# Features of tiles 2 and 3 made and turned in the spatial stage, features of tiles 6 and 7 turned by VectorE: a two-branch mixer in float32 on one core

## The chip, the cores and the metric

The kernel runs on one core of a Trainium2 chip. Its engines are TensorE (PE in the profile; PEld is its weight load), VectorE (DVE), ScalarE (ACT), GpSimd (POOL) and SyncE (SP), which issues most transfers; GpSimd issues some, too. Each engine works its own list of instructions in order. The metric is the device time of one execution in microseconds (us), lower is better, as the median of the runs shown.

## The reference

x is 2048 x 512. Two branches read its layer norm, and their sum is added to x:

```
xn = layernorm(x)
# branch A: 32 heads of width 16
q, k, v = split(xn @ wqkv)
phi_q = concat(softmax(q @ w_phi), softmax(-(q @ w_phi)))       # 32 features for each head; phi_k alike
num = phi_q @ (phi_k^T v);  den = phi_q . sum(phi_k) + 1e-6
A = (num / den) @ wo
# branch B: 688 + 688 features
z1, z2 = gelu(xn @ w_in) split in two;  z2 = layernorm(z2)
g = w_sp @ z2 + b_sp                                            # w_sp is 2048 x 2048, over the sequence
B = (z1 * g) @ w_out
out = x + A + B
```

## The kernel before

Rows of x are cut into 16 tiles of 128 (NT). Every float32 product that must be exact is made of three matmuls: an operand is split into a rounded part (by ScalarE, line 49, or by a copy) and a rest (by VectorE, line 53), and `mm3` (lines 57 to 59) adds high x high, high x low and low x high.

**First stage**: projections, softmax features of q and k for each tile. The unfinished features of q (the exponentials and their sums) go to the DRAM array `e_d`, the first half of branch B to `z1_d`.

**Spatial stage** (its matmuls start between 275.4 and 484.0 us of the span): g = w_sp @ z2. Output rows are done in 8 row pairs i = 0 to 7 (256 rows each), and each pair in four steps over the sequence, so that there are 32 steps n (NC; SEQ gives pair and quarter). A step is a 2x2 block product with seven instead of eight products (FORM: P1 to P7); each is 6 matmuls, 42 in a step, added up over the four steps of a pair in seven PSUM tiles `g` out of a pool of 8. For each step a raw block of w_sp comes in by SyncE (`load_a`, line 607, tile `wf`), and `prep_a` makes its operands `A` from it: ScalarE rounds (line 49), VectorE takes four rests (line 53) and four sums and differences (lines 637 to 640). The operands of steps n and n + 2 share a buffer. At the end of a pair, `drain` adds up the seven products into `c` (lines 834 to 840 on VectorE), and `gate` multiplies by gelu(z1) (line 850 on ScalarE, 853 on VectorE), splits a remainder, and turns the result: VectorE transposes blocks of 32x32 (line 862 twice, line 864), and eight transfers on SyncE (lines 868, 870) store it so that it reads back as whole transposed blocks (`u_d`, `ur_d`). The tile that holds gelu(z1) and then the turned result is `z1t`, one buffer; `c` is one buffer, too. `load_z1` (line 808, GpSimd) fills `z1t` for the next pair.

**Output stage** (to the end): for each pair of tiles TensorE multiplies u by w_out (`project_u`), the features of q by phi_k^T v (`attend`, line 1062, PSUM `po`), and the result by wo (`project_o`). The features of a tile s must be finished first (`q_fin`, lines 563 to 570: a product, a sum over each head, five small steps, a product, all on VectorE) and turned so that features lie on partitions. Turning is done in two ways:

- TensorE transposes (`attend_T`, line 1047, tile `ptq`, 16 for a pair of tiles), and ScalarE copies the result from PSUM (line 1049, four for a pair);
- VectorE transposes blocks (`turn_q`, line 579), four transfers on GpSimd store them to the DRAM array `q_d` (line 581), and SyncE loads them turned (line 1012).

Before, tiles 0 and 1 are finished ahead of the spatial stage (NE = 2), and turned by VectorE in it, behind the gates of pairs 2 and 4 (lines 963 to 968); tile 2 is finished at step 29; tiles 3 to 15 are finished in the output stage (`features`), three tiles ahead of their use. Tiles from TQ = 8 on are turned by VectorE, so that TensorE transposes the pairs of tiles 2 and 3, 4 and 5, 6 and 7.

The code is recorded in program order, and a scheduler sorts the instructions of each engine by a timing of its own; `in_turn` adds an order by hand for the steps at the start of the spatial stage, and `tc.issue_after` holds an instruction behind another one.

## Time and profile before

| | us |
|---|---|
| median of 3 runs (610.21 to 615.73) | 610.74 |
| the profiled execution, its own time | 612.24 |
| its span, from the first to the last instruction | 610.5 |

| engine | busy in the span |
|---|---|
| TensorE | 602.8 us (99%) |
| its weight loads | 548.5 us (90%) |
| VectorE | 525.4 us (86%) |
| ScalarE | 260.3 us (43%) |
| GpSimd | 131.8 us (22%) |

A row of the timeline gives the start in us, the duration (of all that is merged in the row), the engine, the line, the operation, output and input tiles with their shapes, the count, and in brackets the idle time before it and what ended that. Spans of neighbouring instructions on one engine can overlap by up to 0.1 us, so the step from start to start is what an instruction costs in a full queue. An instruction that waits holds all that stands behind it on its engine.

### The profile page before, as it was taken

To read this page: it belongs to the slowest core of one execution; us is meant where nothing else is said; L and a number is where in the kernel's file an instruction comes from. 1 tells how busy PE (TensorE), PEld (TensorE's weight loads), DVE (VectorE), ACT (ScalarE), POOL (GpSimd) and SP (SyncE) were. 2 spreads that over 40 slices of the span, in tenths; PEclk is the share of its full clock that TensorE was granted. 3 is DMA by queue.
4 is the path that set the end of the run, shared out by engine and by line. 5 is a ranking of instruction groups with operands and counts; after the bars stand their busy time and mean duration, and the time that the engine had idled before them with its cause. 6 is when DMAs were issued, how large, how long until landed. Compare 5 with 4: busy or idle time off the path is not lost.

```text
span 610.5 us, 11382 instructions
## 1 busy us (share of the span) xinstructions
PE 602.8 (99%) x4286; PEld 548.5 (90%) x4286; DVE 525.4 (86%) x930; ACT 260.3 (43%) x414; POOL 131.8 (22%) x231
## 2 busy tenths in 40 slices
PE   8999999999999999999999999999999999999997
PEld 7888888888888999999999999999999988877775
DVE  5999999999987578989999897997998999999922
ACT  5643324423433547877434433443435343332220
POOL 4122332323111005442000001001100041153420
PEclk9999999999999999999999999999999999999999
DMA  8557876566537758002344736556664799699782
GB/s 315 193 130 178 217 176 188 145 168 165 144 96 221 241 201 306 5 1 65 121 107 135 208 104 173 163 154 161 176 185 154 228 299 292 191 326 248 183 236 67
DMA packets 57950, 107.85 MB, mean 177 GB/s; under 512 B 12392, under 2 KB 24552, under 8 KB 57672
## 3 DMA queue, kind: packets, MB, share of 16 engines
q1 hardware_dynamic: 43656, 65.22, 34.6%
q0 software_dynamic: 11936, 36.28, 24.2%
q10 hardware_dynamic: 2304, 5.64, 2.4%
q8 instruction: 33, 0.54, 0.4%
q14 instruction: 21, 0.17, 0.1%
HBM read 66.85 MB, written 35.54 MB: 168 GB/s over the span
## 4 chain that ended last, share of the span: by engine, by line
PE 82%; DVE 5%; ACT 4%; issue 4%; POOL 3%; DMA 1%; ACTq 0%; POOLq 0%; DVEq 0%
PE g L57 9%; PE g L59 9%; PE g L58 9%; PE proj L58 7%; PE proj L57 7%; PE proj L59 7%; PE pout L57 5%; PE pout L59 5%; PE pout L58 5%; PE zps L57 3%; PE zps L59 3%; PE zps L58 3%; PE po L1062 1%; DMA et<-e_d 1%; PE kvps L372 1%
## 5 line engine op out<-in xcount | busy, mean ns | idle before, releaser
L57 PE MATMUL g<-B,A 128*128 128x344 f32 x448 | 140.4, 317 | 0.9 <-ACT A L49 0.9
L58 PE MATMUL g<-B,A 128*128 128x344 f32 x448 | 141.1, 317 | 0.0
L59 PE MATMUL g<-B,A 128*128 128x344 f32 x448 | 135.5, 317 | 0.0
L49 ACT ACTIVATE A<-wf 128x512 fp32r<-128x512 f32 (+1 forms) x128 | 69.9, 573 | 109.5 <-DVE wf L639 64.8
L57 PEld LDWEIGHTS g<-B,A 128*128 128x128 f32 x448 | 83.8, 188 | 1.4 <-ACT A L49 1.4
L53 DVE TENSOR_TENSOR A<-wf,A 128x512 fp32r<-128x512 f32 (+1 forms) x128 | 76.5, 619 | 9.8 <-ACT A L49 9.4
L58 PEld LDWEIGHTS g<-B,A 128*128 128x128 f32 x448 | 84.0, 188 | 0.0
L59 PEld LDWEIGHTS g<-B,A 128*128 128x128 f32 x448 | 82.7, 188 | 0.3 <-DVE A L53 0.2
L57 PE MATMUL proj<-wqk_h,xT 128*128 128x512 f32 x128 | 50.1, 391 | 0.0
L59 PE MATMUL proj<-wqk_h,xT 128*128 128x512 f32 x128 | 49.8, 389 | 0.0
L58 PE MATMUL proj<-wqk_l,xT 128*128 128x512 f32 x128 | 49.8, 389 | 0.0
L124 ACT ACTIVATE e<-e,r_x 128x1024 f32<-128x1024 f32 x26 | 29.7, 1148 | 42.2 <-DVE e L123 41.2
L57 PE MATMUL zps<-w1h,xT 128*128 128x344 f32 (+2 forms) x128 | 40.9, 320 | 0.0
L59 PE MATMUL zps<-w1h,xT 128*128 128x344 f32 (+2 forms) x128 | 40.7, 318 | 0.0
L58 PE MATMUL zps<-w1l,xT 128*128 128x344 f32 (+2 forms) x128 | 40.7, 318 | 0.0
L57 PE MATMUL zps<-w2h,xT 128*128 128x344 f32 (+2 forms) x128 | 40.7, 318 | 0.0
L58 PE MATMUL zps<-w2l,xT 128*128 128x344 f32 (+2 forms) x128 | 40.6, 317 | 0.0
L59 PE MATMUL zps<-w2h,xT 128*128 128x344 f32 (+2 forms) x128 | 40.3, 317 | 0.0
L127 DVE TENSOR_REDUCE sm<-e 128x64 f32<-128x1024 f32 x26 | 31.1, 1199 | 2.5 <-ACT e L124 2.5
L808 POOL DMA_DIRECT2D z1t<-z_d x16 | 9.1, 594 | 105.3 <-DVE A L53 38.2
L57 PE MATMUL pout<-wu,uh 128*128 128x512 f32 x75 | 30.4, 406 | 0.0
L59 PE MATMUL pout<-wu,ul 128*128 128x512 f32 x75 | 29.3, 391 | 0.0
(217 smaller groups left out, 1373.0 us busy)
## 6 DMA issues: line engine op xcount, KB each, us to landing
wf<-in_wst SPq DMA_DIRECT2D x64, 256.0 KB, 3.8
e_d<-e POOLq DMA_DIRECT2D x16, 544.0 KB, 4.4
et<-e_d SPq DMA_DIRECT2D x16, 544.0 KB, 7.1
z_d<-z1f ACTq DMA_DIRECT2D x16, 344.0 KB, 2.9
z1t<-z_d POOLq DMA_DIRECT2D x16, 344.0 KB, 4.2
zacc<-e POOLq DMA_DIRECT2D x10, 512.0 KB, 4.8
u<-u_d SPq DMA_DIRECT2D x15, 320.0 KB, 4.9
xt<-in_x SPq DMA_DIRECT2D x16, 256.0 KB, 4.3
```

The lines of the kernel that those rows point to most:

```text
L49: return act.activation(h, src, AF.Copy).ins
L53: return (eng or dve).tensor_tensor(l, src, h.bitcast(F32), op=ALU.subtract).ins
L57: pe.matmul(dst, ah, bh, start=start, stop=False)
L58: pe.matmul(dst, ah, bl, start=False, stop=False)
L59: return pe.matmul(dst, al, bh, start=False, stop=stop).ins
L124: softmax_pair.last = less, act.activation(e, e, AF.Exp, scale=scale).ins
L127: dve.tensor_reduce(sm, heads(e), axis=AX.X, op=ALU.add)
L372: i = pe.matmul(kv_acc[k:k + QP, m // 4], vs[:, m * QP:(m + 1) * QP], e[:, m * HP:(m + 1) * HP], start=first and m < 4 and len(ready) == n ...
L808: pool.dma_start(t[:, k, :FH], z1_d[2 * i + k])
L1062: lasts[3] = pe.matmul(po[r][c * QP:(c + 1) * QP, k], kvT[rows, m // 2, cols], fs[m // 4][rows, m // 2 % 2], start=True, stop=True).ins
```

## The change

- `if 0 < i < 5` in place of `if i in (2, 4)`: behind the gates of pairs 1, 2, 3 and 4 the features of tiles 2, 0, 3 and 1 are turned. Tiles 2 and 3 (s >= NE) are finished there, too: their exponentials are loaded into `c` by GpSimd, and `q_fin` runs with `z1t` as its scratch and with `zs`, a copy of the denominators' sums.
- `zs` takes the third buffer of the raw blocks (`wfy`) from step 6 on; raw blocks from n = 8 on have two buffers, and from n = 6 on `load_a(n + 4)` stands behind `prep_a(n + 2)` in the program.
- TQ = 6: tiles 6 and 7 are turned by VectorE. `ft[2]` is loaded turned, and at step 29 tile 4 is finished instead of tile 2. TensorE then transposes one pair, that of tiles 4 and 5. In the output stage `features` runs from tile 5 on, five tiles ahead.
- `in_turn` gets gate 0's parts, and a second call orders the parts of `prep_a` of steps 8 to 31 one behind another.

```
-    TQ = 8
+    TQ = 6
...
-        tag = "fx"[n] if n < 2 else "fxy"[(n - 2) % 3]
+        tag = "fx"[n] if n < 2 else "fxy"[(n - 2) % 3] if n < 8 else "fx"[n % 2]
...
-        if n + 4 < NC:
+        if n < 6:
             raw[n + 4] = load_a(n + 4)
         if 0 < n < NC - 2:
             A[n + 2] = prep_a(n + 2, raw.pop(n + 2))
+        if 6 <= n < NC - 4:
+            raw[n + 4] = load_a(n + 4)
+        if n == 6:
+            zs = fy[0].tile([P, 2, QC, P], F32, tag="wfy", name="zs").rearrange("p a b c -> p (a b c)")
+            pool.dma_start(zs, zb_d)
...
-                    (4, "A11"), (4, "A22"), (4, "first"), (4, "sums"),
+                    (4, "A11"), (4, "A22"), ("c12", 0), (4, "first"), (4, "sums"),
...
-                    (6, "A11"), (6, "A22"), (6, "first"), (6, "sums"), (6, "S2"), (6, "S4"),
+                    (6, "A11"), (6, "A22"), ("z", 0), (6, "first"), (6, "sums"), (6, "S2"), (6, "S4"),
+                    ("u", 0),
                     (7, "A11"), (7, "A22"), (7, "first"), (7, "sums"), (7, "S2"), (7, "S4"),
+                    ("ut", 0, 0), ("ut", 0, 1),
                     (8, "A11"), (8, "A22"), (8, "first"), (8, "sums"), (8, "S2"), (8, "S4"))
...
-            if i in (2, 4):
-                s = i // 2 - 1
-                e, t = (gt.tile([P, 2, FU], F32, tag=tag, name=name).rearrange("p k f -> p (k f)")[:, :NF]
+            if 0 < i < 5:
+                s = (2, 0, 3, 1)[i - 1]
+                e, t = (gt.tile([P, 2, FU], F32, tag=tag, name=name).rearrange("p k f -> p (k f)")
                         for tag, name in (("c", "c"), ("z1", "z1t")))
-                pool.dma_start(e, e_d[s, :, :NF])
+                t = t[:, :NF]
+                if s < NE:
+                    e = e[:, :NF]
+                    pool.dma_start(e, e_d[s, :, :NF])
+                else:
+                    e, _ = q_fin(load_q(s, e[:, :QW], pool), t, zs)
                 turn_q(s, t, e, pool)
...
-            ets[2] = load_q(2, slot("et"))
-            es[2], last = q_fin(ets.pop(2), slot("qtmp")[:, :NF], zb)
+            ets[4] = load_q(4, slot("et"))
+            es[4], last = q_fin(ets.pop(4), slot("qtmp")[:, :NF], zb)
...
+    in_turn(*((n, k) for n in range(8, NC) for k in ("A11", "A22", "first", "sums", "S2", "S4")))
...
-        ets[3] = load_q(3, slot("et"))
-        for s in (2, 3):
-            us[s] = fetch_u(s)
-        ets[4] = load_q(4, slot("et"))
+        ets[5] = load_q(5, slot("et"))
+        us[2] = fetch_u(2)
+        ft[2] = f_pair()
+        for k in range(2):
+            sp.dma_start(ft[2][:, k], q_d[2 + k])
+        us[3] = fetch_u(3)
+        ets[6] = load_q(6, slot("et"))
...
-        if 3 < i + 3 < NT:
-            features(i + 3)
+        if 0 < i < NT - 5:
+            features(i + 5)
```

From line 849 on the changed kernel's numbers are higher: the gate's 853, 862 and 864 read 854, 863 and 866 there.

**VectorE, behind the gate of pair 1, before.** Here stand the last block of the gate's transposes (L864) and the operands of the next steps, those of two steps mixed:

```order
L864 STREAM_TRANSPOSE z1t<-c 128x192
L639 TENSOR_TENSOR wf<-wf 128x2x128
L640 TENSOR_TENSOR wf<-wf 128x2x128
L53 TENSOR_TENSOR A<-wf,A 128x2x256 x2
L53 TENSOR_TENSOR A<-wf,A 128x256
L637 TENSOR_TENSOR wf<-wf 128x2x128
L53 TENSOR_TENSOR A<-wf,A 128x2x256
L638 TENSOR_TENSOR wf<-wf 128x2x128
L53 TENSOR_TENSOR A<-wf,A 128x256
L639 TENSOR_TENSOR wf<-wf 128x2x128
L637 TENSOR_TENSOR wf<-wf 128x2x128
L640 TENSOR_TENSOR wf<-wf 128x2x128
```

The same place now, from the end of the operands' second difference (L638) on:

```order
L638 TENSOR_TENSOR wf<-wf 128x2x128
L563 TENSOR_TENSOR z1t<-c,zs 128x1024
L639 TENSOR_TENSOR wf<-wf 128x2x128
L564 TENSOR_REDUCE c<-z1t 128x64
L640 TENSOR_TENSOR wf<-wf 128x2x128
L53 TENSOR_TENSOR A<-wf,A 128x2x256
L565 TENSOR_TENSOR c<-c 128x64
L53 TENSOR_TENSOR A<-wf,A 128x2x256
L566 SCALAR_TENSOR_TENSOR c<-c 128x32
L53 TENSOR_TENSOR A<-wf,A 128x2x256
L53 TENSOR_TENSOR A<-wf,A 128x256
L567 RECIPROCAL c<-c 128x32
```

The seven instructions that finish tile 2 have come in between the operands of two steps, the first of them (L563) four instructions into a step's sums.

**VectorE, on to the drain of pair 2.** The rows that follow a little later in the changed kernel; L834 and L837 are the first two steps of the drain of pair 2:

```order
L568 TENSOR_TENSOR c<-c 128x64
L638 TENSOR_TENSOR wf<-wf 128x2x128
L570 TENSOR_TENSOR c<-c 128x1024
L639 TENSOR_TENSOR wf<-wf 128x2x128
L579 STREAM_TRANSPOSE z1t<-c 128x1024
L640 TENSOR_TENSOR wf<-wf 128x2x128
L53 TENSOR_TENSOR A<-wf,A 128x2x256
L834 SCALAR_TENSOR_TENSOR c<-g,bias,c 128x344
L837 TENSOR_TENSOR c<-g,c 128x344
```

All of the finishing and the turning (L579) thus stands ahead of the drain of pair 2, in a stretch where there was nothing of it.

**TensorE, end of the first pair of tiles in the output stage, before** (`ptq` is the PSUM tile of the transposes, `woh` and `wol` are wo, `wu` is w_out):

```order
L57 MATMUL pout<-woh,oT 128x512
L58 MATMUL pout<-wol,oT 128x512
L59 MATMUL pout<-woh,oT 128x512
L1047 MATMUL ptq<-ident,et 128x128 x16
L57 MATMUL pout<-wu,uh 128x512
L58 MATMUL pout<-wu,uh 128x512
L59 MATMUL pout<-wu,ul 128x512
```

and now:

```order
L57 MATMUL pout<-woh,oT 128x512
L58 MATMUL pout<-wol,oT 128x512
L59 MATMUL pout<-woh,oT 128x512
L57 MATMUL pout<-wu,uh 128x512
L58 MATMUL pout<-wu,uh 128x512
L59 MATMUL pout<-wu,ul 128x512
```

The block of 16 transposes is gone here; it is gone, too, behind the pair of tiles 4 and 5, and stays behind that of tiles 2 and 3.

More of the change, by code (lines that the diff above doesn't have):

```diff
@@ L553, in mixer, with load_q @@
     QW = NF + 7 * H
-    def load_q(s, et):
-        sp.dma_start(et[:, :NF + 2 * H], e_d[s])
+    def load_q(s, et, eng=None):
+        (eng or sp).dma_start(et[:, :NF + 2 * H], e_d[s])
         return et
@@ L648, in in_turn @@
         for e in range(2):
-            queue = [turns[k][e] for k in keys if e < len(turns[k])]
+            queue = [turns[k][e] for k in keys if e < len(turns[k]) and turns[k][e]]
             for a, b in zip(queue, queue[1:]):
@@ L844, in drain @@
             turns["c", i, k] = x.ins,
+        turns["c12", i] = None, first.ins
         return cb, first.ins, drained.ins
@@ L849, in gate @@
         with tc.issue_after(after or first):
-            act.activation(z[:, :, :FH], z[:, :, :FH], AF.Gelu_apprx_tanh)
+            turns["z", i] = None, act.activation(z[:, :, :FH], z[:, :, :FH], AF.Gelu_apprx_tanh).ins
         zs = z[:, :, :FH].rearrange("p k (j f) -> p k j f", j=2)
         us = u[:, :, :FH].rearrange("p k (j f) -> p k j f", j=2)
-        dve.tensor_tensor(us, zs, cb, op=ALU.mult)
+        turns["u", i] = dve.tensor_tensor(us, zs, cb, op=ALU.mult).ins,
         lo, hi = u[:, :, KF * P:FH], u[:, :, FH:FU].bitcast(F32R)
@@ L861, in turn @@
             for k in range(2):
-                dve.transpose(m[:, k * KF * P:(k + 1) * KF * P].rearrange("p (m c t) -> p m c t", c=KF, t=BL),
-                              u[:, k, :KF * P].rearrange("p (c m j) -> p m c j", c=KF, j=BL))
+                turns["ut", i, k] = dve.transpose(
+                    m[:, k * KF * P:(k + 1) * KF * P].rearrange("p (m c t) -> p m c t", c=KF, t=BL),
+                    u[:, k, :KF * P].rearrange("p (c m j) -> p m c j", c=KF, j=BL)).ins,
             dve.transpose(r.rearrange("p (k f) -> p k f", k=2), u[:, :, KF * P:])
@@ L1123, in mixer @@
     with tc.issue_after(load_w.last):
-        ets[3] = load_q(3, slot("et"))
-        for s in (2, 3):
-            us[s] = fetch_u(s)
-        ets[4] = load_q(4, slot("et"))
+        ets[5] = load_q(5, slot("et"))
[5 more added lines that the diff above has]
+        ets[6] = load_q(6, slot("et"))
     def ahead(i):
-        if i + 5 < NT:
-            ets[i + 5] = load_q(i + 5, slot("et"))
+        if i + 7 < NT:
+            ets[i + 7] = load_q(i + 7, slot("et"))
         if i + 4 < NT:
-            with tc.issue_after(brought[i + 2]) if i + 6 >= NT else ExitStack():
+            with tc.issue_after(brought[i + 4]) if i + 6 >= NT else ExitStack():
                 us[i + 4] = fetch_u(i + 4)
-        if 3 < i + 3 < NT:
-            features(i + 3)
+        if 0 < i < NT - 5:
+            features(i + 5)
     p, nxt = {}, dict(enumerate(uT))
@@ L1153, in mixer @@
             fin.append(lasts[7])
-            features(3)
+            features(5)
             with tc.issue_after(fin[-1]), tc.issue_after(lasts[8]):
```

## The prediction

> **What bounds the kernel now.** I read the page first, then the queue of TensorE, then stretch by stretch what VectorE has left.
>
> ```profile
> PE 602.8 (99%) x4286; PEld 548.5 (90%) x4286; DVE 525.4 (86%) x930; ACT 260.3 (43%) x414; POOL 131.8 (22%) x231
> ...
> PE g L57 <- ACT A L49: 0.9, 2, 0.6
> ...
> 580.78 1.06 issue
> ```
>
> TensorE is busy 99% of the span. The view of waits finds 0.9 us at two places of the spatial stage, the chain of work 1.06 us at 580.78, ahead of the products with the turned features (L1062). So TensorE is the bound, and what is taken off it is gained, as long as nobody makes it wait instead. The page's 86% for VectorE is a mean over stages; I look at the stage that gets new work. A row pair is four steps of 42 matmuls:
>
> ```profile
> L57 PE MATMUL g<-B,A x448: 313/316/427, 275.4 to 483.7; 128*128 128x344 f32 x150
> ...
> L59 PE MATMUL g<-B,A x448: 313/316/429, 275.7 to 484.0; 128*128 128x344 f32 x150
> ```
>
> These are 3 x 448 = 1344 matmuls between 275.4 and about 484.1 us; less some 1.7 us of gaps that is 0.154 us each, 6.47 us a step and **25.9 us a row pair**. I cut the stage into stretches of 25.9 us, from drain to drain of pairs 1 to 5:
>
> ```profile
> 324.10:350.00 25.90, 25.90 (x170) 25.90 (x169) 24.14 (x53) 12.27 (x22) 1.19 (x3) 1.00 0.57 167
> 350.00:375.90 25.90, 25.90 (x170) 25.90 (x169) 20.22 (x39) 8.32 (x15) 1.86 (x4) 1.00 0.49 133
> 375.90:401.80 25.90, 25.90 (x170) 25.85 (x169) 24.22 (x52) 11.35 (x21) 3.06 (x6) 1.00 0.63 168
> 401.80:427.70 25.90, 25.90 (x170) 25.90 (x169) 21.27 (x41) 9.99 (x19) 2.67 (x5) 1.00 0.54 153
> ```
>
> The fourth number of busy times is VectorE's (behind the length, PE and PEld): 24.14, 20.22, 24.22 and 21.27 of 25.9 us. TensorE never stops here, at a granted clock of 1.00. VectorE has 13.75 us left in 103.6, and even that isn't all free:
>
> ```profile
> 350.32 0.58 DVE L834 SCALAR_TENSOR_TENSOR c<-g,bias,c 128x344 f32<-128x344 f32 x1 [0.70 <-PE g L59]
> ...
> 373.03 1.25 DVE L579 STREAM_TRANSPOSE z1t<-c 128x1024 f32<-128x1024 f32 x1 [3.36 <-DMA wf<-in_wst]
> ...
> 378.14 0.57 DVE L834 SCALAR_TENSOR_TENSOR c<-g,bias,c 128x344 f32<-128x344 f32 x1
> ...
> 402.55 0.57 DVE L834 SCALAR_TENSOR_TENSOR c<-g,bias,c 128x344 f32<-128x344 f32 x1
> ...
> 424.02 1.25 DVE L579 STREAM_TRANSPOSE z1t<-c 128x1024 f32<-128x1024 f32 x1 [2.50 <-DMA wf<-in_wst]
> ...
> 429.13 0.57 DVE L834 SCALAR_TENSOR_TENSOR c<-g,bias,c 128x344 f32<-128x344 f32 x1
> ```
>
> The L834 rows are the first additions of the drains of pairs 2, 3, 4 and 5. At 350.32 VectorE was ahead and waited for TensorE. From there its own stretches are 27.8, 24.4 and 26.6 us. Those of 27.8 and 26.6 hold a turning (L579), before which it stood 3.36 and 2.50 us: the tile `z1t` has to be free of the gate's eight stores, and the exponentials to have come in. The stretch of 24.4 us holds no turning. So VectorE is itself within 2 us of the bound here, and at 378.14 it was 1.9 us behind TensorE's pace (350.32 + 25.9 = 376.2) without stopping it.
>
> **The change, part by part.**
>
> *Off TensorE.* Two of three blocks of transposes go:
>
> ```profile
> 498.76 1.75 PE ptq L1047 x16
> ...
> 531.18 1.75 PE ptq L1047 x16
> ```
>
> That is 2 x 1.75 = **3.5 us** of the chain. The eight copies that ScalarE no longer makes of them cost nothing (it is busy 43%). The 1.06 us at 580.78 go, too: features are finished five tiles ahead instead of three, and VectorE has two finishings fewer in the output stage for two turnings more. **Gain 4.6 us.** The transfers there grow, by my count, by four turned tiles loaded and two stored for two fewer loads of exponentials; between TensorE's use and the landing lies the longer lead, so I cost them at nothing, and at up to 2 us if that cover is too short.
>
> *Onto VectorE.* Finishing a tile is seven instructions:
>
> ```profile
> L563 DVE TENSOR_TENSOR qtmp<-et,zb x16: 1217/1218/1228, 220.0 to 572.9; 128x1024 f32<-128x1024 f32 x16
> L564 DVE TENSOR_REDUCE et<-qtmp x16: 1177/1210/1221, 222.3 to 575.9; 128x64 f32<-128x1024 f32 x16
> ...
> 516.47 1.22 DVE L563 TENSOR_TENSOR qtmp<-et,zb 128x1024 f32<-128x1024 f32 x1
> ...
> 521.24 1.22 DVE L563 TENSOR_TENSOR qtmp<-et,zb 128x1024 f32<-128x1024 f32 x1
> ```
>
> From one tile's first instruction to the next tile's first, with nothing else between, 4.77 us; between other work the gaps are filled, and I take 4.6. The turning adds 1.2 (L579: 1.25, overlapping), and the wait before it is now before L563, which writes `z1t`: it stands about as far behind the gate's transposes as L579 did, so I take the mean of 3.36 and 2.50, 2.9. Against that, the new instructions stand between those of the operands, where some waiting was:
>
> ```profile
> 345.72 0.42 DVE L639 TENSOR_TENSOR wf<-wf 128x256 f32<-128x256 f32 x1
> 346.05 0.42 DVE L637 TENSOR_TENSOR wf<-wf 128x256 f32<-128x256 f32 x1
> ...
> 355.89 0.42 DVE L637 TENSOR_TENSOR wf<-wf 128x256 f32<-128x256 f32 x1
> 356.35 0.43 DVE L638 TENSOR_TENSOR wf<-wf 128x256 f32<-128x256 f32 x1
> ...
> 322.88 1.29 DVE L53 TENSOR_TENSOR A<-wf,A 128x512 fp32r<-128x512 f32 x2 [0.32 <-ACT A L49]
> ```
>
> An instruction that doesn't need the one ahead of it starts 0.33 us after it, one that does 0.46; a step's third rest waits 0.32 us for ScalarE's rounding. Four such gaps of 0.12 and two waits of 0.32 are filled: 1.1 us less. The Trainium skill, page "VectorE: DVE Perf Modes", section "The DRAIN you can't avoid", says that the next operation does not start until the pipe has emptied, and that chaining operations without semaphores wins nothing. The two spacings above differ by 0.13 us, so this trace does not bear it out; by the rule alone the 1.1 would be 0.6, and the sum 1 us higher.
>
> A stretch with finishing and turning (pairs 1 and 3) therefore takes VectorE 24.4 + 4.6 + 1.2 + 2.9 - 1.1 = **32.0 us**. A stretch with a turning alone (pairs 2 and 4) took 27.8 and 26.6, mean **27.2 us**. But in these a wait is new, because the stretch ahead of each now turns, too:
>
> ```profile
> 374.57 2.22 POOL L581 DMA_DIRECT2D q_d<-z1t  x4 [7.66 <-DVE wf L639]
> 381.28 1.10 POOL L808 DMA_DIRECT2D z1t<-z_d  x2 [4.50 <-DMA wf<-in_wst]
> ...
> 387.12 1.34 ACT L850 ACTIVATE z1t<-z1t 128x1376 f32<-128x1376 f32 x1
> ...
> z1t<-z_d POOLq DMA_DIRECT2D x16, 344.0 KB, 4.2
> ```
>
> From the turning's start (373.03) it is 8.3 us to the next issue of gelu's input (381.28), 0.5 to its second half, 4.2 to landing, 1.3 for gelu: 14.3 us. In the changed order there stand between the turning and the gate's multiply the turning itself (1.2), the seven additions of a drain (402.55 to 407.36 in the timeline, less two rests between them: 3.6), the operands of one step and a half (4.4 and 2.4): some 11.7 us. The wait is between 0 and 2.6 us; I take the middle, 1.3 for each of the two stretches. Behind the waiting multiply stand the operands of the next steps, and TensorE waits for those.
>
> Sum: 2 x 32.0 + 2 x 27.2 + 2 x 1.3 = 121.0 us for VectorE where TensorE needs 103.6: **17.4 us too much**. How much VectorE may be late before TensorE stops is not shown, except that 1.9 did no harm. The other end is the PSUM pool: eight tiles, seven of them in use, so a product's tile is written again eight products later, 7.4 us after the product began and 6.5 after it ended (a product takes 0.92), less the 0.57 of L834: 5.9. I take 4.5, nearer the second end, since the first is only what happened to occur; not the whole 5.9, since a step's operands follow each other with less room than the drain has. **TensorE loses 17.4 - 4.5 = 12.9 us.** The two stretches behind pair 4 hold no new work and don't give the time back, since TensorE can't be faster than its matmuls.
>
> Ends of this term: if all other waits of VectorE vanish (13.75 free less 2 x 2.9 standing gives 7.9) the excess is 2 x 4.6 + 2 x 1.2 + 2 x 2.9 - 7.9 = 9.5, less 5.9: a loss of 3.6. If none vanishes, nothing is filled and the multiply waits 2 x 2.6: 17.4 + 5.2 - 1.9 = 20.7.
>
> *Costed at nothing.* Two raw buffers instead of three: a raw block lands 3.8 us after its issue by the page, and the operands of one step in between take 4.4 us (318.50 to 322.88 in the timeline):
>
> ```profile
> wf<-in_wst SPq DMA_DIRECT2D x64, 256.0 KB, 3.8
> ...
> 318.50 2.23 DVE L53 TENSOR_TENSOR A<-wf,A 128x512 fp32r<-128x512 f32 x4 [0.30 <-ACT A L49]
> ```
>
> It is close, and up to 1 us a step where operands follow each other with nothing between; that is in stretches with room. Gate 0's multiply behind later operands may win the 0.9 us of waits near 318, but VectorE is then as late as before; nothing, or -0.9.
>
> Sum for the profiled execution: 612.24 - 4.6 + 12.9 = 620.5 us (its span is 1.7 us shorter). It lay 1.5 us above the median of 610.74, so on the median: **619.0 us**.
>
> **Rivals.**
>
> 1. *VectorE absorbs it; the gain of TensorE stays.* For it: TensorE is at 99% and VectorE at 88% in the four stretches, and 3.36 + 1.2 us too much did no harm in one of them. Against it: the four sums above, with every stretch over 25.9. It decides by whether the excess stays below what may be late, some 5.9 us. The time: 610.74 - 4.6 = 606.1 us, faster. The Trainium skill, page "Perfetto Trace Analysis", section "Identifying the Most-Contended Engine", says to optimize the engine of highest occupancy first; by it this rival wins, and the page's 99% against 86% agree with it as far as they go.
> 2. *It nearly cancels.* The low end of VectorE's term, 3.6 to 7 us lost for 4.6 won: 609.7 to 613.1 us. For it speaks that ScalarE's waits shrink when VectorE is late.
> 3. *Worse than forecast.* Full waits at the multiply, raw blocks late in the catching up as well, nothing tolerated beyond 1.9: 610.74 - 4.6 + 20.7 = 626.8 us.
> 4. *The transposes don't go.* The order of TensorE shows two blocks of 16 fewer, so I give it no chance.
>
> **How the numbers follow.** Forecast 0.60, with its own range of 613 to 625 (a loss of 7 to 19 us); rival 1 0.14; rival 2 0.18; rival 3 0.08. Leaving out rival 3 and most of rival 1 leaves out 2 in 10: the range is 607 to 625 us. A difference of 1% (6.1 us) is about what a measurement of this kernel can tell from no change. Faster by over 1% (below 604.6) lies outside all cases: 0.04. Slower by over 1% (above 616.9) is three quarters of the forecast and rival 3: 0.53. Within 1% remains 0.43.
>
> **What would show it.** In the changed kernel's profile TensorE should have gaps of 5 us and more in all ahead of the drains of pairs 2 and 4 and smaller ones ahead of those of pairs 3 and 5, released by ScalarE's rounding, VectorE's rests or the drain; VectorE should be busy over 95% there, standing about 3 us at L563 twice and at L579 twice, and at the gate's multiply of pairs 2 and 4. The chain of work should show one `ptq` block, and no wait before L1062 at the pair of tiles 12 and 13. I am wrong if TensorE stays gapless to 484 us (then rival 1), if the wait at L563 is below 1 us, or if TensorE waits in the output stage for turned features.

## The result, and the profile after

The changed kernel takes **635.49 us** (median of 5 runs, 635.15 to 636.63), the kernel before on the same chip 611.35 (5 runs, 610.21 to 615.73): a ratio of **1.0388**, 95% interval 1.0362 to 1.0415. It is slower by 24.1 us, where 8.3 were forecast and 625 was the upper end of the range. The profiled execution took 636.63 us, its span 634.9.

The first part of the page (busy time, share of the span), and the view of what TensorE waited for in the spatial stage:

```profile
PE 610.7 (96%) x4254; PEld 549.5 (87%) x4254; DVE 527.9 (83%) x934; ACT 253.3 (40%) x406; POOL 142.8 (22%) x250
```

```profile
PE g L57 <- ACT A L49: 12.6, 11, 2.8
PE g L57 <- ACT c L835: 2.5, 2, 1.8
PE g L59 <- DVE A L53: 0.7, 2, 0.4
```

TensorE, at 99% before, is at 96%. In the spatial stage it now waits 12.6 us at 11 places for ScalarE's rounding of an operand (L49), and 2.5 us for the drain's first copy out of PSUM (L835), where it waited 0.9 us in all before. The next view cuts the stage from the first matmul of a pair to the first of the next (pairs 2 to 7; behind the length stand the busy times of PE, PEld, DVE, ACT and POOL, then the granted clock):

```profile
328.80:356.20 27.40, 26.43 (x170) 25.87 (x169) 23.21 (x48) 9.39 (x17) 1.60 (x3) 1.00 0.49 141
356.20:385.60 29.40, 26.95 (x169) 26.00 (x169) 24.11 (x47) 10.50 (x19) 5.24 (x10) 1.00 0.55 152
385.60:418.70 33.10, 28.68 (x171) 27.34 (x170) 26.57 (x56) 9.49 (x17) 2.48 (x5) 0.95 0.53 155
418.70:447.90 29.20, 26.70 (x170) 26.14 (x170) 22.40 (x44) 9.95 (x18) 3.85 (x7) 0.99 0.57 159
sum 119.10, PE 108.75 PEld 105.36 DVE 96.29 ACT 39.33 POOL 13.18; mean PE 27.19 PEld 26.34 DVE 24.07 ACT 9.83 POOL 3.29
...
447.90:476.40 28.50, 27.74 (x169) 27.17 (x169) 22.28 (x46) 10.02 (x18) 4.39 (x8) 0.95 0.55 146
476.40:510.20 33.80, 29.06 (x170) 27.65 (x169) 29.51 (x58) 15.19 (x28) 0.00 (x0) 0.95 0.67 209
```

A pair that took 25.9 us takes 27.4, 29.4, 33.1, 29.2, 28.5 and 33.8. But VectorE is not at its limit: 96.3 us of 119.1 in pairs 2 to 5, or 81%. The last product ends at 510.4 us, against 484.3 before: **26.1 us later** (the stage begins 0.9 later). The output stage behind it gives back 1.6 us: 124.7 us instead of 126.3. For all the pairs, from the starts of the 1344 matmuls of both traces: the gaps of over 0.4 us hold 17.8 us more than before, matmuls spaced at 0.25 to 0.4 us instead of 0.154 hold 6.4 us more.

VectorE's own waits, from 318 to 515 us:

```profile
DVE A L53 <- ACT A L49: 13.4, 17, 4.2
DVE c L854 <- ACT z1t L851: 6.8, 6, 2.3
DVE z1t L563 <- DMA wf<-in_wst: 6.1, 2, 3.3
DVE z1t L579 <- DMA wf<-in_wst: 2.7, 1, 2.7
```

It stands before the finishing (L563), the turning (L579) and the gate's multiply (L854), about as long as was forecast, and 13.4 us for roundings that ScalarE was late with. (ScalarE waits in its turn, mostly for VectorE's sums, and 13.9 us at six places for raw loads, where before it was 0.2 us at one.) So where does the time go? The chain of work from 337 to 371 us shows it (start, length, what); the row above it is the gate's multiply, with its first and last start in that window:

```profile
L854 DVE TENSOR_TENSOR c<-z1t,c x2: 1591/1592/1593, 337.0 to 370.7; 128x1376 f32<-128x1376 f32 x2
```

```profile
341.94 0.29 DVE z1t L866
...
345.00 3.99 DMA ur_d<-z1t
...
349.27 1.23 DVE z1t L563
...
355.81 1.13 DVE c L570
...
357.28 0.81 DVE z1t L579
...
364.90 0.46 POOL z1t L808
...
365.45 3.62 DMA z1t<-z_d
...
369.33 1.36 ACT z1t L851
370.72 1.59 DVE c L854
```

The stores of the turned tile, one of the steps, aren't in this chain; they are in the row of GpSimd's timeline:

```profile
358.73 2.23 POOL L581 DMA_DIRECT2D q_d<-z1t  x4 [15.35 <-DVE z1t L579]
```

From one gate's multiply to the next are **33.7 us**, and the rows go round two buffers, `c` and `z1t`, that exist once each. Gate and its turning into `z1t` (L866 ends at 342.2): 5.2 us. The gate's stores have to land before `z1t` may be written: to 349.0, 6.8 us. Finishing (L563 to L570, between preparations), to 356.9: 7.9 us. Turning into `z1t`: to 358.4, 1.5 us. The turned tile's stores, until the load of the next gate's input may be issued (L808): 6.5 us. (The chain puts the end of this wait down to a raw load. But L808 waits for the four stores, too: the last of them landed at 364.1 us, and in all four turnings L808 begins 0.6 to 0.8 us after that landing.) That load: to 369.3, 4.4 us. Gelu: 1.4 us. No engine is full in it; it is a ring of steps that wait for each other, longer than the 25.9 us in which TensorE does a pair. With a turning and no finishing it is shorter, in the next pair 27.3 us (370.72 to 398.01). How much of the loss hangs on this ring, the runs below have to show.

### The profile page after: what moved, and what is told of

Read it like the earlier page. It is cut to its first block, busy times and chain, and to the rows that moved or that the text cites. A ratio compares the mean times of both kernels' runs of the same rounds, so it can differ in the third digit from the quotient of the medians.

```text
span 634.9 us, 11370 instructions
## 1 busy us (share of the span) xinstructions
PE 610.7 (96%) x4254; PEld 549.5 (87%) x4254; DVE 527.9 (83%) x934; ACT 253.3 (40%) x406; POOL 142.8 (22%) x250
## 4 chain that ended last, share of the span: by engine, by line
PE 60%; DVE 18%; DMA 13%; issue 4%; ACT 3%; SPq 2%; POOL 0%; DVEq 0%; ACTq 0%; POOLq 0%
PE proj L58 7%; PE proj L57 7%; PE proj L59 7%; DMA wf<-in_wst 6%; PE zps L59 6%; PE zps L58 6%; PE zps L57 6%; PE g L57 3%; PE g L59 3%; PE g L58 3%; DVE A L53 3%; PE pout L57 3%; PE pout L59 3%; PE pout L58 3%; DMA u<-u_d 2%
## 5 line engine op out<-in xcount | busy, mean ns | idle before, releaser
L57 PE MATMUL g<-B,A 128*128 128x344 f32 x448 | 144.8, 326 | 15.1 <-ACT A L49 12.6
L49 ACT ACTIVATE A<-wf 128x512 fp32r<-128x512 f32 (+1 forms) x128 | 66.6, 569 | 122.6 <-DVE wf L639 101.0
L57 PEld LDWEIGHTS g<-B,A 128*128 128x128 f32 x448 | 85.6, 191 | 19.5 <-ACT A L49 15.8
L53 DVE TENSOR_TENSOR A<-wf,A 128x512 fp32r<-128x512 f32 (+1 forms) x128 | 74.3, 617 | 18.3 <-ACT A L49 18.0
L58 PEld LDWEIGHTS g<-B,A 128*128 128x128 f32 x448 | 85.9, 192 | 0.0
L59 PEld LDWEIGHTS g<-B,A 128*128 128x128 f32 x448 | 81.8, 191 | 2.5 <-DVE A L53 2.4
L127 DVE TENSOR_REDUCE sm<-e 128x64 f32<-128x1024 f32 x26 | 31.1, 1198 | 2.5 <-ACT e L124 2.5
L581 POOL DMA_DIRECT2D q_d<-qtmp x40 | 22.6, 577 | 37.7 <-DVE qtmp L579 37.7
L59 PE MATMUL pout<-wu,ul 128*128 128x512 f32 x75 | 29.3, 390 | 0.0
```

Source lines behind the costliest of these rows:

```text
L49: return act.activation(h, src, AF.Copy).ins
L53: return (eng or dve).tensor_tensor(l, src, h.bitcast(F32), op=ALU.subtract).ins
L57: pe.matmul(dst, ah, bh, start=start, stop=False)
L58: pe.matmul(dst, ah, bl, start=False, stop=False)
L59: return pe.matmul(dst, al, bh, start=False, stop=stop).ins
L127: dve.tensor_reduce(sm, heads(e), axis=AX.X, op=ALU.add)
```

## The experiments

Theories, as they came up. **RING**: the lost third raw buffer. **WORK**: VectorE's added instruction time, as forecast. **ORDER** and **LIST**: TensorE's new order of products, and the list that causes it. **TURNS**: the two turnings more with their waits, whatever the list. **WAIT**: VectorE's in-order queue held ahead of finishing and turning. **CHAIN** (first called CYCLE): the ring of steps through `c` and `z1t`, some of which are transfers. Each time stands beside runs of the kernel before on the same chip, whose medians were 611.2 to 611.9 us.

### Undoing and doing single parts

The raw ring of two alone, on the kernel before:

```diff
-        tag = "fx"[n] if n < 2 else "fxy"[(n - 2) % 3]
+        tag = "fx"[n] if n < 2 else "fxy"[(n - 2) % 3] if n < 8 else "fx"[n % 2]
 ...
-        if n + 4 < NC:
+        if n < 6:
             raw[n + 4] = load_a(n + 4)
         if 0 < n < NC - 2:
             A[n + 2] = prep_a(n + 2, raw.pop(n + 2))
+        if 6 <= n < NC - 4:
+            raw[n + 4] = load_a(n + 4)
```

> The kernel before, with one part of the change alone: from step 8 on the raw row blocks go round two buffers instead of three, so that a block's load is issued only after the block two steps earlier has been read. Nothing is finished or turned in addition. If the lost third buffer is what costs (theory RING), VectorE's ordinary work should already run into late loads: 615 to 628 us, with TensorE gaps that end on wf<-in_wst in pairs 2 to 7. If VectorE's added finishing and its waits cost (theory WORK), the loads land in time as the prediction said: 611 to 613 us. If TensorE's new product order costs (theory ORDER), 611 to 612, since its order is here nearly that of before.

620.9 us, ratio 1.0159 (1.0137 to 1.0182). ScalarE's and TensorE's waits in its spatial stage:

```profile
ACT A L49 <- DMA wf<-in_wst: 49.5, 21, 5.3
...
PE g L57 <- ACT A L49: 3.7, 4, 1.9
PE g L59 <- DVE A L53: 1.6, 1, 1.6
```

ScalarE waits for raw loads at 21 places (0.2 us at one place before), and TensorE for ScalarE. By itself this edit, which the prediction costed at nothing, costs **9.4 us**, in the band of RING. But that is not the change's price. Three raw buffers again in the changed kernel, the copy of zb gone from the third:

```diff
-        tag = "fx"[n] if n < 2 else "fxy"[(n - 2) % 3] if n < 8 else "fx"[n % 2]
+        tag = "fx"[n] if n < 2 else "fxy"[(n - 2) % 3]
 ...
-                    e, _ = q_fin(load_q(s, e[:, :QW], pool), t, zs)
+                    e, _ = q_fin(load_q(s, e[:, :QW], pool), t, e[:, :NF])
```

> The kernel after, with three raw buffers as before. The buffer that held the copy of zb is a raw buffer again, and the finishing of tiles 2 and 3 multiplies e by e itself in place of zb (these two tiles' features are then other numbers; the instructions, shapes and waits on VectorE stay, only the load of the copy of zb goes). TensorE's order of products is that of after but for a handful. RING: most of the loss goes, 617 to 622 us, with no chain rows of wf<-in_wst. WORK: 631 to 636, since VectorE's work is the same. ORDER: 631 to 636.

634.7 us, 1.0372 (1.0346 to 1.0397): giving the third buffer back wins nothing measurable. RING is refuted as the cause in the change: the price of two buffers doesn't add to that of the rest. In the next two the finishing goes:

```diff
-                    e, _ = q_fin(load_q(s, e[:, :QW], pool), t, zs)
+                    e = load_q(s, e[:, :QW], pool)[:, :NF]
```

> The kernel after, with two raw buffers, but tiles 2 and 3 are loaded and turned without being finished (left out: the seven instructions of the finishing, about 4.6 us on VectorE a tile; their features are unfinished). RING: the loads stay late, 622 to 633 us. WORK: 609 to 614, since two turnings more (1.2 us each) are all that is left. ORDER: 625 to 636, since TensorE's order is the interleaved one throughout.

620.65 us, 1.0153 (1.0126 to 1.0180).

> Both at once: three raw buffers, and tiles 2 and 3 turned without being finished. RING and WORK: 607 to 612 us, below or at the kernel before by the 3.5 us of transposes that went. ORDER: 622 to 636, since the interleaved order of products is the same as with two buffers.

622.5 us, 1.0185 (1.0156 to 1.0213). The finishing costs 14.8 us with two raw buffers and 12.2 with three; some 9 to 11 us stay without it, in both. No theory had both numbers. Next the list, alone on the kernel before, and out of three variants of after:

```diff
+    in_turn(*((n, k) for n in range(8, NC) for k in ("A11", "A22", "first", "sums", "S2", "S4")))
```

> The kernel before, with the other part of the change alone: the list that fixes, for steps 8 to 31, the order A11, A22, first, sums, S2, S4 of VectorE's and ScalarE's preparations, one step behind the other. Three raw buffers, two turnings, nothing finished in addition. LIST (the list takes from VectorE the preparations that it made a step ahead, and each wait of its queue reaches TensorE): 616 to 624 us, the loss in the pairs in which a turning's load is waited for (3 and 5). TURNS (two more turnings with a wait of about 3 us each are what the run without finishing lost): 610 to 613.

613.5 us, 1.0033 (1.0020 to 1.0047): 1.6 us, though TensorE's order is then nearly as interleaved as in the changed kernel (a matmul of line 57 directly behind one of line 58, with line 59 put off: 94 times; 42 before, 111 in the changed kernel). ORDER falls, and LIST misses its band.

> The kernel after with three raw buffers, tiles 2 and 3 turned but not finished (their finishing is left out), and without the list for steps 8 to 31. LIST: 607 to 612 us, about 11 to 15 below the run with the list. TURNS: 618 to 623, as with the list.

618.5 us, 1.0104 (1.0089 to 1.0119), the lower end of the band of TURNS: of 11 us above before some 4 were the list's, the rest is there without it.

> The kernel after with three raw buffers (the finishing of tiles 2 and 3 multiplies e by itself in place of the copy of zb, so their features are other numbers) and without the list for steps 8 to 31, the finishing kept. LIST: the finishing's 9 us of VectorE and its waits fall into the lead, 612 to 620 us. If the finishing costs its 12 us whatever the list: 619 to 624. TURNS: 630 to 636.

632.95 us, 1.0363 (1.0328 to 1.0398), in the band of TURNS.

> The kernel after, but without the list for steps 8 to 31: two raw buffers, finishing kept, nothing left out. LIST and RING together: with two buffers VectorE cannot run a step ahead either, so 622 to 632 us. LIST alone: 612 to 620. TURNS: 632 to 638.

635.1 us, 1.0373 (1.0350 to 1.0395): the same, and LIST falls as well. Without ring and list 21 of the 24 us are still there, and they go with the finishing (14.4 us, 632.95 against 618.5) and with the two turnings more (6.7 us above before, although 3.5 us of transposes are gone).

### Work, wait or chain

The finishing's instructions alone, on the kernel before:

```diff
             if i < NP - 2:
                 turn()
+            if i in (1, 3):
+                e = c.rearrange("p k f -> p (k f)")
+                q_fin(e[:, :QW], e[:, :NF], e[:, :NF])
```

> The kernel before, with the finishing's seven instructions run twice more on VectorE, after the gates of pairs 1 and 3, as in after, on what the dead buffer c then holds (their results are used by nothing). No load, no wait, no z1t, three raw buffers. CYCLE: VectorE has room for it, 611 to 614 us. WORK: the 12 to 15 us that the finishing cost in after come with it, 621 to 627.

612.6 us, 1.0006 (0.9987 to 1.0025): **nothing**. The stretch from 301.8 to 432.4 us, first of before, then of this kernel (the third busy time is VectorE's):

```profile
301.80:432.40 130.60, 129.72 (x839) 128.90 (x838) 114.95 (x236) 53.09 (x93) 9.86 (x19) 1.00 0.54 150
```

```profile
301.80:432.40 130.60, 129.79 (x839) 129.23 (x839) 117.16 (x243) 51.42 (x92) 9.80 (x18) 1.00 0.51 143
```

Fourteen instructions were added, but only seven more stand in the stretch: VectorE prepares seven instructions' worth less ahead of need, and TensorE is as busy as before. The lead takes up 9.2 us of work. The same with waits and no work:

```diff
+            if i in (1, 3):
+                e = gt.tile([P, 2, FU], F32, tag="c", name="c").rearrange("p k f -> p (k f)")
+                pool.dma_start(e[:, :NF + 2 * H], e_d[i // 2 + 2])
+                dve.tensor_copy(e[:, QW:QW + 2], e[:, :2])
```

> The kernel before, with two more loads of e into the dead buffer c, after the gates of pairs 1 and 3, each followed on VectorE by one tiny copy (128x2) that waits for it. So VectorE's queue is held at four places, as in after, but nothing is finished, turned or stored in addition, and z1t is not touched. WAIT (a held VectorE queue is what costs): the run that turned all four tiles without finishing, three buffers, no list, was 6.7 us above before; these two waits of some 3 us bring as much, 615 to 619 us. CHAIN (the chain through c and z1t): VectorE's lead covers a wait, 611 to 613.

612.8 us, 1.0029 (1.0015 to 1.0042): 1.6 us for two waits, in the band of CHAIN. The test is weaker than it was meant to be: in the trace the two copies waited 2.0 us together, where the two finishings waited 6.1. Of the theories, the chain is left. First its part between the turning and the next gate, by a buffer of its own for the turned `e` in the changed kernel, with two raw buffers and the list (the second run leaves out the finishing, too):

```diff
-                t = t[:, :NF]
+                t = fy[0].tile([P, 2, QC, P], F32, tag="wfy", name="own").rearrange("p a b c -> p (a b c)")
```

> The kernel after, but e is turned (and the finishing's products are made) in the buffer that held the copy of zb, and no longer in z1t; the finishing multiplies e by itself in place of zb, so tiles 2 and 3's features are other numbers. Two raw buffers and the list stay, and so does all of VectorE's work. CYCLE (one chain goes round the two buffers c and z1t in each pair: gate, turning, the stores of the turned gate, finishing, turning of e, its stores, the load of the next z1t, gelu, the next gate; in after from gate to gate 33.7, 27.3 and 34.6 us where a pair has 25.9): the stores of e and the load of z1t leave the chain, some 11 of 33.7 us; the pairs 3 to 5 that took 28 to 33 us take 26 to 28, and the whole 616 to 625 us. WORK (VectorE's added work and its waits cost in themselves): 630 to 636 us.

627.3 us, 1.0247 (1.0213 to 1.0281): 8.2 us less, all of VectorE's work being still there; two over the band of CHAIN, and below that of WORK.

> The same buffer for the turned e, with tiles 2 and 3 turned and not finished (their finishing is left out); two raw buffers, list kept. CYCLE: without it the pairs 2 to 5 took 27 to 28 us each; they come down to 26 to 26.5, and the whole from 620.7 to 611 to 616 us. WORK: no difference, 619 to 622.

619.8 us, 1.0123 (1.0089 to 1.0157), 0.9 us less: a miss for CHAIN, and in the band of WORK. The run without the finishing had no such wait before the buffer was changed (VectorE's waits from 300 to 515 us):

```profile
DVE c L854 <- ACT z1t L851: 2.8, 6, 0.5
```

The gate's multiply stood 2.8 us in all, 0.5 at the longest, so the chain was not what held there. What did is open: two raw buffers cost 9.4 us alone, but the same kernel with three took 622.5 us. With three buffers and no list:

```diff
-                turn_q(s, t, e, pool)
+                if s < NE:
+                    turn_q(s, t, e, pool)
+                else:
+                    dve.transpose(t.rearrange("p (m c t) -> p m c t", c=NB, t=BL), e.rearrange("p (c m j) -> p m c j", c=NB, j=BL))
 ...
-            sp.dma_start(ft[2][:, k], q_d[2 + k])
+            sp.dma_start(ft[2][:, k], q_d[k])
```

> The run with three raw buffers, without the list and without the finishing (618.5 us), and in it the turned tiles 2 and 3 are not stored (the output stage loads the rows of tiles 0 and 1 in their place, so two tiles' features are others). The load of the next z1t then waits for the turning alone and no longer for the stores of the turned e. CHAIN: some 6 us leave the chain in pairs 2 and 4, all pairs take 26 us again: 611 to 614. WAIT or WORK: the loads of e, their waits and the turnings are the same, 617 to 619.

613.3 us, 1.0039 (1.0019 to 1.0060): the turnings' 6.7 us above before become **2.1** when two tiles' stores leave the chain. (The profiled execution took 618.2 us, some 5 of them lost in the output stage; its spatial stage alone is read.) VectorE's waits from 300 to 460 us, first with these stores, then without:

```profile
DVE c L854 <- ACT z1t L851: 7.2, 4, 3.6
```

```profile
DVE c L854 <- ACT z1t L851: 2.5, 5, 0.8
```

The gate's multiply now waits at most 0.8 us for gelu and its input, and VectorE's turnings and their loads are the same. Here CHAIN met its band. Next, the time ahead of the finishing (its operand in place of the load, its products in place of `z1t`):

```diff
+                e = c.rearrange("p k f -> p (k f)")
+                t = gt.tile([P, 2, FU], F32, tag="z1", name="z1t").rearrange("p k f -> p (k f)")[:, :NF]
-                if s < NE:
-                    e = e[:, :NF]
-                    pool.dma_start(e, e_d[s, :, :NF])
-                else:
-                    e, _ = q_fin(load_q(s, e[:, :QW], pool), t, e[:, :NF])
+                if s >= NE:
+                    q_fin(e[:, :QW], e[:, :NF], e[:, :NF])
+                e = e[:, :NF]
```

> The kernel after with three raw buffers and without the list (632.95 us), with all of VectorE's finishing and turning, but without any wait ahead of it: the four loads of e are left out and the finishing works in place on what c holds (so tiles 0 to 3's features are other numbers); the turning still goes into z1t. CHAIN: the 7 us between the gate's turning and the finishing leave the chain, 33.7 becomes about 27 in the pairs with a finishing and 27.3 about 23 in the others: 612 to 619. WORK: VectorE does the same work, 628 to 634. WAIT: 612 to 616.

629.3 us, 1.0295 (1.0273 to 1.0316): 18.1 us above before instead of 21.1, a miss for CHAIN as I had worked it out, and for WAIT, whose waits are gone; it lies in the band of WORK. The trace shows what took the place of the wait: the finishing began 5.5 us earlier than in the kernel that it was cut from (341.7 us for 347.2), but its seven instructions were then spread between preparations over 12.0 us instead of 8.8, and from gate to gate were still 33.6 us (334.95 to 368.50) for 35.3. The chain had hardly become shorter, and the time hardly did. So VectorE's preparations between the steps of a finishing belong to the length of the ring, too. Last, all stores of turned tiles out of the chain, the finishing left as it is:

```diff
-                turn_q(s, t, e, pool)
+                dve.transpose(t.rearrange("p (m c t) -> p m c t", c=NB, t=BL), e.rearrange("p (c m j) -> p m c j", c=NB, j=BL))
```

> The kernel after with three raw buffers and without the list (632.95 us), the finishing kept with its loads, waits and place in VectorE's queue, but none of the four turned tiles is stored: the output stage loads rows of e as they were in their place, so tiles 0 to 3's features are others. The load of the next z1t waits for the turning alone. CHAIN: 6 us leave the chain in every pair, 33.6 becomes about 27.6 with a finishing and 27.5 about 21.5 without, so that a pair of both has 49 against 51.8 us and the lead covers the longer one: 611 to 617 us. WORK (VectorE's finishing and turning where they stand): nothing of that changes, 628 to 634.

624.95 us, 1.0219 (1.0198 to 1.0240): 8.0 us less, which lies between the bands of WORK and CHAIN. From the matmul starts, pairs 2 to 7 take 25.8, 33.9, 26.5, 31.1, 26.0 and 25.8 us: nearly all the loss is in pairs 3 and 5, into which the finishings reach. In the kernel that this one was cut from, the same pairs took 25.8, 31.8, 30.8, 28.9, 28.6 and 29.3. Pairs 2 to 5 are 117.3 us in both: without the stores nothing is won there, and the 6 us that the spatial stage wins are in pairs 6 and 7. (The buffer of its own was alike: 3 us less in pairs 2 to 5, 8 in pairs 6 and 7, in the profiled executions.) The waits of TensorE and ScalarE there, and a part of the chain:

```profile
PE g L57 <- ACT c L835: 7.9, 2, 4.5
...
ACT c L835 <- DVE z1t L977: 8.0, 3, 3.7
```

```profile
356.87 1.13 DVE c L570
358.00 1.20 DVE A L53 x2
359.20 1.17 DVE z1t L977
360.37 0.02 issue
360.39 0.47 ACT c L835
```

L977 is the turning. ScalarE's first copy of the next pair's drain writes `c`, and waits 8.0 us in three places until the turning has read the finished tile out of it; TensorE waits 7.9 us for that copy, since the next product's PSUM tile is free only with it. That is the second ring, through `c` alone: load, finishing and turning hold it until the drain wants it. These 7.9 us, and some 25 matmuls at half speed behind them (3.3 us; see the last section), are most of the 13.2 us that pairs 3 and 5 lose. That it also sets the loss of pairs 2 to 5 in the changed kernel itself is not shown: no run cut this ring, and there TensorE waits more for roundings (12.6 us) than for this copy (2.5). With the buffer of its own it waits only 0.7 us for the copy, and pairs 2 to 5 still lose 12.

### Versions

Four turnings after pairs 0, 2, 4 and 5, with the finishing moved ahead of the stage:

```diff
-    NE = 2
+    NE = 4
 ...
-            if 0 < i < 5:
-                s = (2, 0, 3, 1)[i - 1]
+            if i in (0, 2, 4, 5):
+                s = (0, 2, 4, 5).index(i)
```

> A version that keeps the chain short: tiles 2 and 3 are finished like 0 and 1 ahead of the spatial stage (VectorE is busy 11.5 of 20 us there in the kernel before), all four tiles are only turned there, after pairs 0, 2, 4 and 5, three raw buffers, no list; the output stage is that of after. CYCLE: a pair with a turning has a chain of 27.3 us, one without is shorter, so the alternate pairs make it up, and after pair 5 nothing waits for the next gate until the end: 606 to 611 us, the gain of the transposes less what the finishing costs ahead. If each turning costs its 2 us wherever it stands (WORK): 614 to 620.

638.3 us, 1.0432 (1.0392 to 1.0471), far outside both bands.

```profile
PE zps L57 <- ACT z L776: 11.9, 3, 8.8
```

The two finishings held up the stage ahead (its `zps` products wait 11.9 us), and pair 0 begins at 291.1 us instead of 275.4. Room in a window of 20 us wasn't room at the place. The spatial stage itself is 11.3 us longer than before, too, mostly in pairs 0 and 2 (31.4 and 30.8 us); that wasn't taken apart. Then the parts that the chain doesn't touch (the edits to `in_turn`, `drain` and `gate` and gate 0's keys as in the change's diff, here with one line more):

```diff
-    TQ = 8
+    TQ = 6
```

> A version with the two cheap parts of the change alone: gate 0's places in the list of steps 1 to 8, and the output stage's tiles 6 and 7 turned by VectorE instead of TensorE (the constant 8 becomes 6). The spatial stage of before is otherwise unchanged. Gate 0's places took 1.7 us out of pair 1 in the traces of after (27.6 to 25.9 us); one block of 8 transposes is 1.75 us. If both come through: 608 to 609 us. If the output stage gives its part back in waits, as in after, 609 to 610.5.

618.9 us, 1.0128 (1.0098 to 1.0159), where 608 to 610.5 were expected.

```profile
PE po L1066 <- DMA f<-q_d: 7.6, 2, 4.7
```

TensorE waits 7.6 us at two places for turned features to be loaded back; in the chain their loads land at 538.6 and at 574.9 us. They come too late with the three tiles of lead that this version has; the change has five. And gate 0's places alone:

> The kernel before with one part of the change alone: gate 0's drain, gelu, multiply and turning get places in the list that orders steps 1 to 8. Pair 1 took 27.57 us in the profile of before and 25.9 us in the traces of kernels with these places; if nothing else moves, 609.5 to 611 us.

610.74 us, **0.9982** (0.9971 to 0.9994): 1 us faster than before, the best kernel here. Pair 1 takes 25.9 us instead of 27.6, pair 3 gives back 1.2.

## Why the prediction was wrong, point by point

- **The step that failed** is "Sum: 2 x 32.0 + 2 x 27.2 + 2 x 1.3 = 121.0 us for VectorE where TensorE needs 103.6", and with it "The two stretches behind pair 4 hold no new work and don't give the time back", which puts their loss at nothing. The sum adds VectorE's instructions and waits as if its queue were the bound. VectorE was busy 96.3 of 119.1 us in these four pairs, and the finishing's work alone cost nothing (1.0006). The waits in that sum, which I had listed one by one (2.9 ahead of L563, 8.3 from a turning to the next issue of gelu's input, 4.2 for its landing, 1.3 for gelu), were links of one chain; adding them to each other, instead of to VectorE's work, gives its length. The 14.3 us that I worked out from turning to gate and set against the instructions in between should have been set against the pair: with 5.2 for gate and turning, 6.8 for the stores and 7.9 for the finishing it makes 34 us, and 33.7 were measured.
- **Where the number went wrong.** From the starts of the same matmuls in both profiled executions: in the four stretches (324.1 to 427.7 us before) TensorE lost 13.2 us, where 12.9 were forecast. In the two behind them it lost another 12.9, forecast as nothing, and the output stage gave back 1.6 instead of 4.6. These two make up the 16 us that the forecast lacked. That the 12.9 came out in the four stretches is luck as far as the runs show, since VectorE's added work by itself stops nothing there. Of the 12.9 us behind, 6.1 are left with three raw buffers and without the list, and none when the stores are out of the ring as well. So there the ring through the stores is shown. In the four stretches the loss goes with the finishing (7.0 us without it and 13.7 with it, three raw buffers, no list) and doesn't go with the stores (13.8; of the 7.0 without the finishing, 1.3 are left when two tiles aren't stored). Through what the finishing holds TensorE up there is read from the rows above only in part, and stays open.
- **"How much VectorE may be late", 4.5 us**: too small where only work is added: 9.2 us of it stopped nothing. VectorE then has fewer preparations made ahead; that this, and not the PSUM tiles, sets the limit is read from the counts of instructions and not tested.
- **Two raw buffers, costed at nothing**: alone 9.4 us. The price was hidden in the change (634.7 against 635.5 us), so this error didn't show in the total, but the step was wrong. I had compared the load with one step's operands; I now think that the time for which a block is held has to be added, which no run tests.
- **The list for steps 8 to 31** wasn't costed at all: 1.6 us alone on the kernel before; of the 11 us above before without the finishing, some 4.
- **The granted clock**, taken as 1.00: it was 0.50 in three stretches, which cost some 4 us (see the last section).
- **TensorE's gain, 4.6 us**: the output stage became 1.6 us shorter. Of three blocks of transposes one is left and the wait of 1.06 us is gone, as forecast, but VectorE's rests (2.0 us) and ScalarE (0.2) are new waits there. The remaining 0.8 us weren't traced.

```profile
L1062 PE MATMUL ptq<-ident,et x16: 271/273/273, 540.3 to 541.9; 128*128 128x128 f32 x16
```

```profile
PE pout L59 <- DVE oT L53: 2.0, 3, 0.9
PE pout L57 <- ACT xr L1119: 0.2, 1, 0.2
```

- **Right**: the sign; that TensorE gets gaps, and whom it waits for in them (rounding, drain, rests); 3 us at L563 twice (6.1). At L579 it was one wait instead of two. Not right: VectorE "over 95%" busy (77 to 85%), and gaps up to pair 5 only; pairs 6 and 7, with no turning of their own, lost 10.6 us.
- **Slips that change little**: VectorE's share in the four stretches is 87%, not 88 (89.85 of 103.6 us). The upper end of the loss counts the multiply's 2.6 us twice and leaves out the 2.2 us of gaps that it says aren't filled: 20.3 us instead of 20.7.
- **Rivals**: the first (VectorE absorbs it) was right about VectorE's work and wrong about the time. By the Trainium skill, "Perfetto Trace Analysis", section "Identifying the Most-Contended Engine", the engine of highest occupancy comes first (for TensorE that section goes not by the matmuls' busy share but, among others, by that of the weight loads: 90% here against VectorE's 86%, which chooses the same), so taking work off TensorE should have won; this case shows the limit of that rule. The same page, section "Optimization Strategy", says that the same gap repeating on the engine that should be saturated can mean that there isn't room for the next tile. That is the sentence that fits: the gaps repeat pair by pair, and `c` and `z1t` exist once.

## What to carry to other kernels

When new work is put into a loop, add up the round trip of every buffer that it borrows (write, use, store, landing, reload, next use), and compare it with one turn of the loop; busy shares and sums of instructions don't show it. In this kernel work that VectorE could do from what it had cost nothing, since it had a lead, while the same work behind a load and ahead of a store, in buffers that the next turn needs, cost 14 us. Cutting one ring won nothing in the pairs where something else held TensorE as long. Look behind the stretch that gets the new work, too: what is late there may be late further on. And a part that is costly alone may be free in the sum, so that giving it back wins nothing.

## What the hardware showed that was not expected

After gaps TensorE ran slow for a while. In the changed kernel's trace the granted clock is 0.50 three times in the spatial stage, from 413.26, 447.40 and 498.60 us on, for 3.41 us each. These starts lie 34.1 and 51.2 us apart, which is 10 and 15 times 3.41. So I cut the trace into pieces of 3.41 us on that grid; here are the three slow pieces, each with the one ahead of it, and two others (behind the length stands PE's busy time, behind the five busy times the granted clock):

```profile
399.61:403.02 3.41, 2.97 (x20) 2.69 (x18) 3.41 (x9) 0.00 (x0) 0.00 (x0) 1.00 0.00 0
403.02:406.44 3.42, 2.12 (x14) 2.12 (x14) 3.09 (x7) 1.98 (x4) 0.54 (x1) 1.00 0.89 186
409.85:413.26 3.41, 1.37 (x9) 1.09 (x9) 2.51 (x3) 0.63 (x1) 0.00 (x0) 1.00 0.12 45
413.26:416.68 3.42, 3.42 (x12) 3.05 (x13) 3.38 (x10) 1.46 (x3) 0.00 (x0) 0.50 0.08 22
443.99:447.40 3.41, 1.63 (x11) 1.35 (x10) 1.13 (x2) 1.05 (x2) 0.00 (x0) 1.00 0.88 272
447.40:450.81 3.41, 3.41 (x14) 3.41 (x13) 3.38 (x9) 0.46 (x1) 2.21 (x4) 0.50 0.35 70
495.19:498.60 3.41, 1.56 (x8) 1.27 (x9) 2.96 (x6) 2.37 (x5) 0.00 (x0) 1.00 0.99 334
498.60:502.01 3.41, 3.41 (x14) 3.41 (x13) 3.26 (x6) 0.98 (x2) 0.00 (x0) 0.50 0.94 290
```

In a slow piece matmuls follow each other in 0.287 us instead of 0.154. Ahead of each stands a piece in which TensorE was idle for 1.8 to 2.0 us of 3.41. The gaps in them were 2.35, 2.10 and 3.11 us from start to start of two matmuls. But gaps of 2.09 and 2.06 us in the same trace were followed by no slow piece, nor were three of 2.6 to 3.3 us in the changed kernel without the list: they lie across a border of the grid. The second of them is shown above, with 0.4 us of idle time on one side and 1.3 on the other. In the 20 traces of this case, leaving out the first 20 and the last 10 us of each, there are 25 slow stretches of one, two or three such pieces. Within a trace all begin on one grid, and each begins behind a piece with 1.6 us of idle time or more; behind a piece with over 1.85 us the clock was always halved, and in between it sometimes was. So by these traces it isn't the length of a gap that decides, but the idle time in a fixed piece of 3.41 us, with a limit near half of it.

The Trainium skill, "TensorE: Matmul & The Clock Gate", section "Why this matters for your kernels", advises against idle gaps of over some 3 us, since a window of idleness halves the clock. Here the halving came after gaps of 2.1 us as well, so the advice is too generous for this kernel.
